# One pool of eight buffers for streamed weights and pair sums, free order of block products, and a new order of all steps

## The chip, the cores and the metric

The kernel runs on one core of a Trainium2 chip. The time is that of the core on the device, in microseconds (us), as the median of several executions. One further execution is recorded by the hardware profiler; all rows below come from that one.

## The reference

Eight batches of eight heads: 512 local rows that see a window of 32 to each side and 32 global rows, and 32 global rows that see everything. The result, as 4352 rows of 512, goes through an MLP with a gelu.

```python
k_all = np.concatenate([k_g, k_l], axis=2)
v_all = np.concatenate([v_g, v_l], axis=2)
s_g = scale * np.matmul(q_g, k_all.transpose(0, 1, 3, 2))
out_g = np.matmul(sm(s_g), v_all)
s_ll = scale * np.matmul(q_l, k_l.transpose(0, 1, 3, 2))
...
s_ll = np.where(mask, s_ll, -1000000000.0)
s_lg = scale * np.matmul(q_l, k_g.transpose(0, 1, 3, 2))
s_l = np.concatenate([s_lg, s_ll], axis=-1)
a_l = sm(s_l)
out_l = np.matmul(a_l, np.concatenate([v_g, v_l], axis=2))
return np.concatenate([out_g, out_l], axis=2).astype(np.float32)
...
h = x @ w_in
inv_sqrt2 = np.float32(1.0 / np.sqrt(2.0))
g = 0.5 * h * (1.0 + erf(h * inv_sqrt2))
return (g @ w_out).astype(np.float32)
```

Here `sm` is the softmax over the last axis, `w_in` is 512 x 2048 and `w_out` 2048 x 512.

## The kernel before

**Attention** is cut into 64 units: a batch, a half of its local rows, a pair of heads. A unit loads keys, queries and values (`load_k`, `load_q`, `load_v`: tiles `raws` and `vr`), transposes keys and queries, multiplies them on TensorE (`s`, line 906), masks and reduces on VectorE (line 925), takes the exponential on ScalarE (line 779, tile `a_t`), normalizes (`n`, tile `ge`), transposes the weights on TensorE (`t`, lines 980 to 983), copies them (`at`) and multiplies them by the values (`o`, line 1017). The global rows run beside it (`sg`, `gt`, `go`, `gx`, tiles `sgr`, `agt`, `gos`; their values come by `gu_load`, lines 1131 and 1133). Numbers of fp32 are cut into a high and a low part, so that a product is three matmuls: high by high, high by low, low by high. The low part is a subtraction, mostly on GpSimd (line 612).

**The MLP** takes 256 rows at a time: 16 chunks (a batch's half each) and one of all global rows. The first five are plain. The last twelve go in six pairs (index `k`), whose first layer is done by seven products of half-size blocks instead of eight (`i` = 1 to 7), for each quarter of the hidden columns (`q` = 0 to 3): 168 products, each of 12 matmuls of 128 x 256 (`ml_p`, line 1314, tile `hb`). The sums of weight blocks that the products want are made once (`sw`, `ss`, `sh`, `sl`), and written to DRAM with the plain blocks (`wd`, one tensor for each quarter). Each product then streams its weights back: step `rl` (`r_l`, line 1275) loads 128 x 1024 numbers into a tile `rt`, which is free again when the product has read it. Partial sums stand in PSUM (W, X, Y of a quarter); `cc` adds two of them into a tile `gq` for the gelu (line 779), and `gl`, the low part of the gelu's result, is the last to use it. The second layer (`mo`, lines 1360 to 1362, tile `acc`) adds up in two PSUM banks, and `ob` and `ow` copy and store the result.

**Buffers.** Sixteen large tiles of one pool hold half of the weights' high parts for good (eight) and serve as two rings of four: `rg` for `rt`, `gq` for pair sums (line 229). A ring hands out its oldest free buffer.

**What sets the order.** `graph()` names 4431 steps, each with what it needs, the buffers it takes and frees, and the engines that may run it. The order of all steps, and the engine of each, was found beforehand by a search and stands packed in the text `SEQ`: two bytes for a step, its number times six plus the engine. `plan()` unpacks it, and the loop at the end issues the steps in that order; each engine runs its own instructions in the order in which they are issued. The due times and the table `DUR` matter only to the search. Nearly all loads and stores are issued by SP (SyncE) in one queue; an instruction of SP that waits for a buffer holds all behind it. The products stand in a fixed order: each needs the one before it (`prev`, line 509), and each `rl` stands behind the one before it (`rprev`).

```python
ORDER = [(0, 1), (1, 1), (0, 2), (2, 1), (1, 2), (3, 1), (2, 2), (3, 2)] + [(q, i) for q in range(4) for i in (6, 5, 7, 3, 4)]
```

Of the kernel before, what the change touches and what calls it, by code (L numbers as in the profile page):

```python
# [139 lines left out]
FORMS = (3, 5, 7, 9, 11, 15, 19, 23, 27, 32)  # L140
# [17 lines left out]
    "8dM-oF@Ik0as!Mfq^Y{8xQr!93hIeiD8r{-%$CJA<2#y;=`OtLy3b2o8q+*{{G|tgmY&x8AL{_{F&S;5o#*zE|)UaeMuT{dydLa19s3J@ln;eMD3J&3b_UCeBfR-hUTIZ*}?o{yOwO^}^OD{vEKlo`Z)F9^r"
    "ua0`8Ju(>j4TTt5~^LbK3Ne6AircmvOE?Zo2=pMfcau)m5^v|jgP@ZI&c*0^7Y_q3W?1NDK{_Ieh<Oc3L<_%Fc|aew&@crIZwQHgisqpbmas$NI<3EWqoXw9}3@fkla(2H*({0c7mC)EF!=puYvKefKxItec"
    "hC<){7{q_BX7+^l}MS?0YrgebWkH7C<Km@ef@Pqgdi2L!c)~~JC1=bMf*N<-<sNYooE`AYlJKh{9l9u9!@t@$|uJ;pG5Z!^r^^;q-)Q1VX@f+|Ph(F-@;2rh80I0RUwU4x!@I2|;`pv``VFz({E2?!XemAj7"  # L160
    "I$Zw~{uKUYf|PujFq8BpVPET6e2TEYejjlHDI6#e#u5&-RtcB!2Z^r}Is=!8$6H?@?IO$}4YZ!9SCjQ*K54Y|EO8=Xc56CtuJsze5I9D3l7A<J$)m*E_<1A?`2l{2<Rgy_EGG2^mXp3Bfhi&Yg3?49A;ifyi"
    "1P_Ugq5UEN%LASw;mvzB-|n1Cdfz+h-V1z6E>2L5-^k-t$_N+#JhwqNFNi12@?ZU3Y>%`EodDf2`D<!{{<cq))C~yBNQNsNFq=cwK7OcTiL|_22x};1xSPtrIaFhW$OuwfLJB(C;dn=lGe1Uh!e<f2GGP&%7"
    "K85bey!Il|VdCdO2{Jax8F%GLHO^bdEAgIvKdr+CsWY`h(O?sv(C+4_fb%UL(H~cs-CJH4{GwtfuZG&jGEY-k^ZVO3Iejvw<hAFO#Q|ceFmB7%6^=jk1yIp$wA2fro+L0toW803y&u*-6Eb{|qq6B}%pCUSJ"
    "`aPo6;r1b-lZKpsQ+kqim$r%nW;g7_ddKp`(DuOgof{*O!vZl!J}M<^c#z9j!l{+2qPa+=Hv{!UI%c9Cz9CsU44FOVNo7(^g&8U;+9L0L(=9sD@3KJYjB1IjBD1ob$TK>dhvnmUj27KIcL(HQ{?QB9ZA_XDC"
    "pEOim(evnSRK$TIg^l{Yb0083#^)KqBppY7%KMk&?@PkG=m-<KWIqEvfrhuEcBk*-#UjV{*NWDs(ND~JilRb1TbqX~=R0d7dDE%q*bIOdMJ~%7*4JAz6K|wJ7kLsk77#?bXIybnF@-b~Ht(Ha%p=g~%E+bCQ"
    "QQN5%>Hrf@%Mw8$EMpvfFt`+$qB0l*)EP8Oa5j}n%hDONrA&Be5}h7;gNh3|X-%{tsw>E)i5M%HH-HO+O4@8@KfO#BhTfx&q3dW;#!T9Bs)hCn-NRTC^atlMwTyRYuhEv!-ej()nHYn#R@z2dg?IuKqP<98$"
    "ec&NK??_Yp&&yRTFs2nVvKljKf}TJlJ+YtP20rW#auui4))MS=zr1<GZxXu(WbC2(u%Zo%w4o4^!qejXqcV}ZexB<|Ad}n>|rJutAqQQJLnte&7tq<_Rw_J0BeNyI_m_Z7(76$Fb>gwqE~|#nB#&IgVTcRg1"
    "OMEp+3eU)@;`1pb6w+za4sxaf<E>9c7+k9;H2``Prki$BZ+~WuY_lw^*w}lNn1{A@--CVCX%@C3-*OHvJ98ON`%{A2Qw#Z3}J+%@6Gg*3c`V8}uQ@*w8R*4x>E;qoe2#=ua6*b~?0%wSl!IRAJLNG4>YLj?h"
    "ZR?$Ex_8phwu3*bYc;~^7kPw-&y5%Ve-$hrxJGVQE-`VXwn7{^$5!CM*sfMK;c_E(IfK{xAEki((TVJtxH`)$vLMj1g?9Sc)?o`I{~#u{PVV&Yk&AvWs|#wcrAh)W-CyUOTe-(~PQ0v3gJE~MZ{SpRFg98$B"
# [379 lines left out]
def attn_mlp(ctx, tc, q_l, k_l, v_l, q_g, k_g, v_g, w_in, w_out, out):  # L549
# [918 lines left out]
```

## Time and profile before

| | us |
|---|---|
| median of 3 runs | 1015.15 (1011.89 to 1018.85) |
| profiled execution | 1016.96 |
| its span, first to last instruction | 1015.2 |
| TensorE busy (PE) | 987.0, 97% |
| VectorE busy (DVE) | 745.0, 73% |
| ScalarE busy (ACT) | 715.9, 71% |
| GpSimd busy (POOL) | 444.9, 44% |

PE is matmuls, PEld the loading of their stationary side, SPq the queue of SyncE, which issues DMAs. A wait is idle time of an engine ahead of an instruction, put down to what ended last before it. The chain of waits follows the last instruction back, at each step to what released it. The granted clock is the share of TensorE's full clock that the chip gave it.

### The profile page before, as it was taken

How to read it: one execution, taken by the hardware profiler on the slowest of the kernel's cores; microseconds unless marked ns; L12 is line 12 of the kernel's file. 1: busy time of each engine (PE TensorE's matmuls, PEld its weight loads, DVE VectorE, ACT ScalarE, POOL GpSimd, SP SyncE). 2: the span in 40 equal slices, each digit the busy share in tenths (PEclk: the TensorE clock that was granted, in tenths of full speed). 3: DMA queues.
4: the chain of work that ended last, by engine and by line, in shares of the span. 5: the costliest groups of instructions: out<-in, count | busy, mean ns of one | idle time of the engine just before them, and what ended most of it. 6: DMA issues, size and time to landing. Idle time of an engine off the chain costs nothing.

```text
span 1015.2 us, 21336 instructions
## 1 busy us (share of the span) xinstructions
PE 987.0 (97%) x6712; PEld 865.3 (85%) x6712; DVE 745.0 (73%) x2184; ACT 715.9 (71%) x1703; POOL 444.9 (44%) x473
## 2 busy tenths in 40 slices
PE   7999999999999999999998999999999999999998
PEld 5767688998998888888897988888899979988986
DVE  5888999888898999788886886689888876231110
ACT  5888868778877688787776877777787766433231
POOL 6331657434344464244542464335533553325132
PEclk9999999999999999999999999999999999999999
DMA  9996322445545888876677657875678846754831
GB/s 216 291 273 153 65 49 45 110 89 156 130 89 154 241 242 267 239 195 147 179 211 204 140 141 197 235 210 139 176 201 244 218 96 200 247 167 122 265 113 42
DMA packets 307729, 175.06 MB, mean 172 GB/s; under 512 B 256256, under 2 KB 279040, under 8 KB 307616
## 3 DMA queue, kind: packets, MB, share of 16 engines
q1 hardware_dynamic: 304064, 171.07, 63.3%
q0 software_dynamic: 1344, 1.97, 0.7%
q8 instruction: 54, 0.88, 0.4%
q10 hardware_dynamic: 2208, 0.66, 0.3%
q14 instruction: 59, 0.48, 0.2%
HBM read 149.49 MB, written 24.12 MB: 171 GB/s over the span
## 4 chain that ended last, share of the span: by engine, by line
PE 71%; DMA 14%; DVE 8%; SPq 3%; ACT 2%; issue 2%; POOL 0%; DVEq 0%; ACTq 0%; POOLq 0%
PE hb L1314 18%; PE acc L1360 9%; PE acc L1361 9%; PE acc L1362 9%; DMA rt<-wd 4%; PE o L1017 4%; PE s L906 4%; PE h L1206 2%; PE h L1210 2%; PE t L980 2%; PE h L1211 2%; PE h L1212 2%; PE acc L1352 2%; DMA raws<-in_v_l_dram 2%; DMA raws<-in_q_l_dram 2%
## 5 line engine op out<-in xcount | busy, mean ns | idle before, releaser
L1360 PE MATMUL acc<-wh,gh 128*128 128x512 f32 x512 | 205.1, 401 | 0.0
L1361 PE MATMUL acc<-wh,gl 128*128 128x512 f32 x512 | 200.8, 392 | 1.1 <-POOL gl L612 1.0
L1362 PE MATMUL acc<-wl,gh 128*128 128x512 f32 x512 | 200.6, 392 | 0.0
L612 POOL TENSOR_TENSOR gl<-gf,gh 128x512 fp32r<-128x512 f32 x80 | 105.3, 1316 | 204.8 <-ACT gh L605 48.6
L1314 PE MATMUL hb<-fh,rt 128*128 128x256 f32 x960 | 183.4, 282 | 5.9 <-DMA rt<-wd 4.7
L1314 PEld LDWEIGHTS hb<-fh,rt 128*128 128x128 f32 x960 | 152.6, 189 | 10.4 <-DVE sm L925 2.6
L1314 PE MATMUL hb<-fl,rt 128*128 128x256 f32 x480 | 134.3, 280 | 0.0
L779 ACT ACTIVATE a_t<-a_t,sm 128x192 f32<-128x192 f32 (+1 forms) x256 | 117.1, 460 | 11.2 <-DVE sm L931 10.4
L1362 PEld LDWEIGHTS acc<-wl,gh 128*128 128x128 f32 x512 | 96.2, 188 | 21.1
L1360 PEld LDWEIGHTS acc<-wh,gh 128*128 128x128 f32 x512 | 96.7, 189 | 16.0 <-ACT ob L605 0.6
L1361 PEld LDWEIGHTS acc<-wh,gl 128*128 128x128 f32 x512 | 96.6, 189 | 16.1 <-POOL gl L612 1.7
L612 POOL TENSOR_TENSOR vs<-vr,vs 128x512 fp32r<-128x512 f32 x56 | 73.8, 1319 | 83.2 <-DVE k L612 13.0
L779 ACT ACT_TABLE_LOAD x69 | 88.5, 1283 | 16.2 <-PE acc L1362 6.5
L1314 PEld LDWEIGHTS hb<-fl,rt 128*128 128x128 f32 x480 | 90.4, 188 | 1.1
L925 DVE CUSTOM_DVE_ANT_0 a_t<-s,mask 128x192 f32<-128x192 f32 (+1 forms) x256 | 81.8, 366 | 11.0 <-PE s L906 10.2
L612 POOL TENSOR_TENSOR gl<-gq,gh 128x512 fp32r<-128x512 f32 x47 | 63.4, 1349 | 52.9 <-PE acc L1362 22.0
L605 ACT ACTIVATE at<-t 128x512 fp32r<-128x512 f32 (+1 forms) x112 | 59.0, 542 | 26.8 <-PE t L981 10.5
L1000 DVE TENSOR_TENSOR at<-t,at 128x512 fp32r<-128x512 f32 (+1 forms) x112 | 67.3, 615 | 14.0 <-ACT at L605 13.2
L1210 PE MATMUL h<-xh,wh 128*128 128x256 f32 x256 | 74.0, 289 | 0.9 <-DVE agt L1116 0.9
L1314 PE MATMUL hb<-xf,rt 128*128 128x256 f32 x576 | 74.8, 281 | 0.0
L1017 PE MATMUL o<-at,vs 128*128 128x256 f32 x448 | 70.3, 287 | 2.3 <-ACT sgr L779 1.6
L1314 PEld LDWEIGHTS hb<-xf,rt 128*128 128x128 f32 x576 | 71.1, 189 | 1.4
(196 smaller groups left out, 2348.0 us busy)
## 6 DMA issues: line engine op xcount, KB each, us to landing
rt<-wd SPq DMA_DIRECT2D x168, 512.0 KB, 4.6
wraw<-in_moe_w_in_dram SPq DMA_DIRECT2D x16, 512.0 KB, 6.1
wraw<-in_moe_w_out_dram SPq DMA_DIRECT2D x16, 512.0 KB, 6.2
raws<-in_v_l_dram SPq DMA_DIRECT2D x64, 128.0 KB, 4.0
out_dram<-ob SPq DMA_DIRECT2D x32, 256.0 KB, 3.0
raws<-in_k_l_dram SPq DMA_DIRECT2D x224, 36.0 KB, 2.8
raws<-in_q_l_dram SPq DMA_DIRECT2D x224, 32.0 KB, 3.1
vr<-in_v_l_dram SPq DMA_DIRECT2D x48, 128.0 KB, 4.1
```

What stands on the lines that cost most here:

```text
L605: nc.scalar.activation(out=out, in_=in_, func=AF.Copy)
L612: (nc.vector if e == "v" else nc.gpsimd).tensor_sub(**kw)
L779: nc.scalar.activation(func=func, **kw)
L906: nc.tensor.matmul(out=st[u, "s", jj][:, c:c + w], lhsT=qq[pr, qt * P:qt * P + P], rhs=kk[pr, k0:k0 + w], start=(i == 0 and n == 0), stop= ...
L925: nc.vector.tensor_tensor_reduce(out=a_t[:, j, aoff[half][i]:aoff[half][i] + w], in0=s[:, c:c + w], in1=masks[half][i], scale=1.0, scalar= ...
L1000: nc.vector.tensor_sub(out=at[:, 1], in0=st.pop((u, "t", j))[:, :n * P].rearrange("p (n q) -> p n q", q=P), in1=at.bitcast(F32)[:, 0])
L1017: nc.tensor.matmul(out=o[:, :, qsl], lhsT=l.rearrange("p s e -> p (s e)"), rhs=r, start=(n == 0), stop=(n == 3), skip_group_check=True)
L1210: nc.tensor.matmul(out=h, lhsT=hi, rhs=xh, start=(c == 0 and f % 2 == 0), stop=False, skip_group_check=True)
L1314: nc.tensor.matmul(out=h[:, r], lhsT=a, rhs=b, start=(i in (1, 5) and r == 0 and c == 0 and n == 0), stop=(c == 1 and n == 2), skip_group_ ...
L1360: nc.tensor.matmul(out=acc[t], lhsT=gh[:, f % 2, tsl], rhs=hi, start=(f == 0), stop=False)
L1361: nc.tensor.matmul(out=acc[t], lhsT=gl[:, f % 2, tsl], rhs=hi, start=False, stop=False)
L1362: nc.tensor.matmul(out=acc[t], lhsT=gh[:, f % 2, tsl], rhs=lo, start=False, stop=(f == NF - 1))
```

## The change

Four things. The two rings become one of eight buffers, `rg`, for the streamed weights and the pair sums (and for the weight sums before them). The products no longer need one another, nor the loads of weights, so that any order may be chosen in which each product has its data and its partial sums; those of a pair may overlap those of the next. Most loads and stores may be issued by SP or by GpSimd (`by(e)`). And the order of all steps is searched anew, with load times that were measured; of the text `SEQ` one line of each is shown. In the new order SP issues as many DMAs as before, 1350, and GpSimd none more. `FORMS` says which of the smaller tiles lie in which of two pools. `graph()` and the table `DUR` are otherwise as they were.

```diff
-FORMS = (3, 5, 7, 9, 11, 15, 19, 23, 27, 32)
+FORMS = (0, 1, 3, 11, 15, 19, 23, 25, 27, 32)
...
-    "c-jrriDME3<1k<bj2i}w`yMc0+&7H-8ZcnM7~>lE81tQGrl!8jpDi;pGh4RI%+#itnXj6fnVOj`H8nLgwPjv;rDkfTrl#Nb{1J}@YKInJqtF1<1LZ@%h9;pRXgl-@^f>f9Gz+ajWzat81ZWm^1FD6-3cU*j1"
...
+    "c-jrriDMFk;s9XAeP81m_kaQ8hH(uTFkrxd0b`77++%D{&6b(^me1BQGc#MZXJ%$LeP+wIY?+xYGh1qEYHHJ#&nq?4WoD+ProZ3!M|?Jz1(t*RU<sH2_5~~r7sFhzR@e#H6buYV!+wU9VCP|S*bG=NY#MeC{"
...
-    bufs = {"s": 2, "t": 2, "h": 2, "gg": 5, "u": 6, "sm": 4, "wr": NF, "fw": NF + 1, "rg": 4, "gq": 4}
+    bufs = {"s": 2, "t": 2, "h": 2, "gg": 5, "u": 6, "sm": 4, "wr": NF, "fw": NF + 1, "rg": 8}
...
-        rk = "gq" if g // 4 else "rg"
+        rk = "rg"
...
-            step(("ya", n), "y_a", (n,), "s", 270.0 + n, [("w5", n), ("w5", wl[-1])], [], [("fw", ("lo", n)), ("gq" if grp // 4 else "rg", ("H", grp))], issues=2, size=0.5)
+            step(("ya", n), "y_a", (n,), "sp", 270.0 + n, [("w5", n), ("w5", wl[-1])], [], [("fw", ("lo", n)), ("rg", ("H", grp))], issues=2, size=0.5)
...
-            step(("lv", u), "load_v", (u, 2), "s", f0 - 18.0, [("o", units[n - 2], 1)], [("vr0", u), ("vr1", units[n + 1])], issues=9, size=0.5, after=("lv", pu if n == NPV else units[n - 2]))
+            step(("lv", u), "load_v", (u, 2), "sp", f0 - 18.0, [("o", units[n - 2], 1)], [("vr0", u), ("vr1", units[n + 1])], issues=9, size=0.5, after=("lv", pu if n == NPV else units[n - 2]))
...
-                step(("glv", g, i), "gu_load", (g, i), "s", g0 - 12.0 + 2 * i, [("tk", units[NPE - x]) for x in (3, 4)], [("gvr", (g, i))], issues=6, size=0.33, after=("glv", *pi) if pi[0] else None)
+                step(("glv", g, i), "gu_load", (g, i), "sp", g0 - 12.0 + 2 * i, [("tk", units[NPE - x]) for x in (3, 4)], [("gvr", (g, i))], issues=6, size=0.33, after=("glv", *pi) if pi[0] else None)
...
-        prev = ("P", k - 1, 3, 4) if k else ("hc", keys[NPL - 1], NF - 1, NCC - 1)
-        rprev = ("rl", k - 1, 3, 4) if k else None
...
-            step(("rl", k, q, i), "r_l", (k, q, i), "s", Q - 9.0, w, [("rg", (k, q, i))], issues=1, size=0.52, after=rprev)
-            rprev = ("rl", k, q, i)
-            step(("P", k, q, i), "ml_p", (k, q, i), "t", Q, [prev, ("rl", k, q, i), ("fl", k, i)] + more, [W[q]] if i == 1 else [Y[q]] if i == 5 else [],
-                 [("rg", (k, q, i))] + ([] if q < 3 else [("xx%d" % x, (k, "F")) for x in (2 * i - 2, 2 * i - 1)] if i < 3 else [("fw", ("F", k, i, x)) for x in range(2)]))
-            prev = ("P", k, q, i)
+            step(("rl", k, q, i), "r_l", (k, q, i), "sp", Q - 9.0, w, [("rg", (k, q, i))], issues=1, size=0.52)
+            step(("P", k, q, i), "ml_p", (k, q, i), "t", Q, [("rl", k, q, i), ("fl", k, i)] + more, [W[q]] if i == 1 else [Y[q]] if i == 5 else [],
+                 [("rg", (k, q, i))] + ([("xx%d" % x, (k, "F")) for x in (2 * i - 2, 2 * i - 1)] if i < 3 else [("fw", ("F", k, i, x)) for x in range(2)]))
...
-                step(("se", k, q), "ml_se", (k, q), "a", Q - 1.0, [("sd", k, q), ("P", k, q - 1, 3) if q else ("P", k, 3, 2)], [X[q]], [("s1%d" % q, k)])
+                step(("se", k, q), "ml_se", (k, q), "a", Q - 1.0, [("sd", k, q)], [X[q]], [("s1%d" % q, k)])
...
-                step(("cc", k, q), "ml_cc", (k, q), "v", Q + 1.5, [("P", k, q, 7), ("qc", k, q)], [("gq", (k, q))], [("q", (k, q))])
+                step(("cc", k, q), "ml_cc", (k, q), "v", Q + 1.5, [("P", k, q, 7), ("qc", k, q)], [("rg", (k, q))], [("q", (k, q))])
...
-                step(("gl", key, f), "ml_gl", (key, f), "v" if key == "g" and f == NF // 2 - 1 else "p", d + 1.3, [("gh", key, f)], [("gl", (key, f))], [("gq", (k, q)) if bh else ("gf", (key, f))])
+                step(("gl", key, f), "ml_gl", (key, f), "v" if key == "g" and f == NF // 2 - 1 else "p", d + 1.3, [("gh", key, f)], [("gl", (key, f))], [("rg", (k, q)) if bh else ("gf", (key, f))])
...
-    spare = {"fw": [2 * NF - 1], "rg": [], "gq": []}
+    spare = {"fw": [2 * NF - 1], "rg": []}
...
+    def by(e):
+        return {"a": nc.scalar, "p": nc.gpsimd, "s": nc.sync}[e]
...
-            st["S", g] = room("gq" if g // 4 else "rg", ("S", g), [P, 4, CH], F32, "ss")
+            st["S", g] = room("rg", ("S", g), [P, 4, CH], F32, "ss")
...
-        nc.sync.dma_start(out=t.bitcast(F32), in_=wd[q][:, FORM[i]])
+        by(e).dma_start(out=t.bitcast(F32), in_=wd[q][:, FORM[i]])
...
-        st["gq", k, q] = t = room("gq", (k, q), [P, 2, 2, CH], F32, "gq")
+        st["gq", k, q] = t = room("rg", (k, q), [P, 2, 2, CH], F32, "gq")
```

The table `SEQ` sets the order; two places show what it does.

SP's queue at the loads for the fourth quarter (`wd3`) of the second pair. Among them stand `raws` (keys, line 726, and queries, line 731; with lines 1131 and 1133 values for the global rows). Before, with `rt_7891` for product 6, `rt_8039` for product 5 and the others for 7, 3 and 4:

```order
L1275 DMA rt_7889<-wd2_125 128x1024
L1275 DMA rt_7891<-wd3_126 128x1024
L726 DMA raws_142<-in_k_l_dram 32x9x32 x4
L1131 DMA raws_142<-in_v_l_dram 128x4x64 x2
L1133 DMA raws_142<-in_v_g_dram 32x2x64 x4
L1275 DMA rt_8039<-wd3_126 128x1024
L731 DMA raws_142<-in_q_l_dram 32x8x32 x4
L1275 DMA rt_8053<-wd3_126 128x1024
L1275 DMA rt_8074<-wd3_126 128x1024
L1275 DMA rt_8101<-wd3_126 128x1024
```

After, with `rt_7852` for product 5, `rt_7908` for product 6, and `wd0` for the first weights of the next pair:

```order
L1274 DMA rt_7852<-wd3_126 128x1024
L1274 DMA rt_7854<-wd2_125 128x1024
L730 DMA raws_142<-in_q_l_dram 32x8x32 x4
L1274 DMA rt_7908<-wd3_126 128x1024
L725 DMA raws_142<-in_k_l_dram 32x9x32 x4
L1274 DMA rt_8076<-wd3_126 128x1024
L1274 DMA rt_8085<-wd3_126 128x1024
L730 DMA raws_142<-in_q_l_dram 32x8x32 x4
L1274 DMA rt_8137<-wd0_123 128x1024
L1181 DMA xg_136<-gc_8053 128x32
L1274 DMA rt_8169<-wd3_126 128x1024
```

The weights of product 5 stood behind four loads of keys and six of values for the global rows, and now stand first of their quarter; of values nothing stands among them any more, and weights of the next pair come ahead of the quarter's last.

ScalarE's queue at the last unit of attention, where the exponentials (`a_t`, `sgr`) and the gelus (`gf`, `gq`) alternate. Before:

```order
L779 ACTIVATE gf<-hb 128x512
L779 ACT_TABLE_LOAD
L779 ACTIVATE a_t_128,sm<-a_t_128,sm 128x192
L779 ACTIVATE a_t_128,sm<-a_t_128,sm 128x224
L779 ACTIVATE sgr_132,gsm<-sgr_132,gsm 128x544
L605 ACTIVATE vs<-vr 128x8x64
L605 ACTIVATE hb<-s_5278 128x512
L779 ACTIVATE a_t_128,sm<-a_t_128,sm 128x192
L779 ACTIVATE a_t_128,sm<-a_t_128,sm 128x224
L779 ACT_TABLE_LOAD
L779 ACTIVATE gf<-hb 128x512
```

After:

```order
L778 ACT_TABLE_LOAD
L778 ACTIVATE gf<-hb 128x512
L601 ACTIVATE hb<-s_5316 128x512
L601 ACTIVATE q<-hb 128x512
L601 ACTIVATE gh<-gf 128x512
L778 ACT_TABLE_LOAD
L778 ACTIVATE sgr_132,gsm<-sgr_132,gsm 128x544
L601 ACTIVATE xf<-xb 128x256 x2
L778 ACT_TABLE_LOAD
L778 ACTIVATE gq<-hb 128x512
L778 ACTIVATE gf<-hb 128x512
```

Exponentials that stood in one run between two table loads are now cut by a gelu, which makes three table loads in eleven rows instead of two. Over the whole kernel ScalarE has 80 table loads instead of 70, and VectorE 2223 instructions instead of 2186 (casts of `gh` and low parts of weights above all, taken from ScalarE and GpSimd).

## Rows read from the trace of the kernel before

**Rows 1.** Page, part 1: busy us (share of the span) x instructions, by engine

```profile
PE 987.0 (97%) x6712; PEld 865.3 (85%) x6712; DVE 745.0 (73%) x2184; ACT 715.9 (71%) x1703; POOL 444.9 (44%) x473
```

**Rows 2.** Busy us (x instructions) by stage: PE, PEld, DVE, ACT, POOL, clock, DMA

```profile
0.00:150.00 150.00, 140.11 (x815) 105.73 (x816) 123.36 (x362) 118.92 (x288) 67.55 (x110) 1.00 0.69 176
150.00:350.00 200.00, 199.84 (x1449) 180.98 (x1449) 176.29 (x516) 154.47 (x380) 95.08 (x98) 1.00 0.49 121
350.00:850.00 500.00, 487.05 (x3457) 435.67 (x3456) 410.91 (x1233) 386.80 (x924) 231.01 (x227) 1.00 0.74 195
```

**Rows 3.** Waits of TensorE, 350 to 850 us: total us, times, longest

```profile
PE hb L1314 <- DMA rt<-wd: 4.7, 5, 2.1
PE t L980 <- ACT gq L779: 1.9, 1, 1.9
PE o L1017 <- ACT sgr L779: 1.6, 1, 1.6
PE acc L1361 <- POOL gl L612: 1.0, 1, 1.0
PE gx L1166 <- DVE gos L1161: 0.8, 1, 0.8
PE t L980 <- ACT gf L779: 0.8, 2, 0.6
```

**Rows 4.** Streamed weights' tile rt: issue ns min/median/max; landing us

```profile
L1275 SPq DMA_DIRECT2D rt<-wd x168: 319/371/1643, 334.5 to 971.9; - x168
...
DMA to landing us min/median/max: 3.4/4.6/7.7
```

**Rows 5.** Waits of SP's queue, whole span: total us, times, longest

```profile
SPq L1275 <- PE hb L1314: 110.8, 71, 10.5
```

**Rows 6.** Chain of waits, 524 to 556 us: start us, us, what

```profile
538.39 7.12 DMA rt<-wd
...
546.90 3.87 DMA rt<-wd
```

**Rows 7.** Timeline, 538 to 552 us: start us, us, what [idle before, releaser]

```profile
540.94 0.63 ACT L605 ACTIVATE vs<-vr 128x512 fp32r<-128x512 f32 x1 [3.06 <-DMA rt<-wd]
...
541.59 1.28 ACT L779 ACT_TABLE_LOAD   x1
...
542.88 0.60 ACT L779 ACTIVATE gq<-hb 128x512 f32<-128x512 f32 x1
543.01 3.79 SPq L1133 DMA_DIRECT2D raws<-in_v_g_dram  x4
...
543.53 0.44 PE L980 MATMUL t<-ident,a_t 128*128 128x128 f32 x2 [1.86 <-ACT gq L779]
...
546.90 0.37 SPq L1275 DMA_DIRECT2D rt<-wd  x1
...
550.90 0.36 PE L1314 MATMUL hb<-fh,rt 128*128 128x256 f32 x1 [2.06 <-DMA rt<-wd]
```

**Rows 8.** Busy us by single microseconds from 552; clock is behind POOL

```profile
552.00:553.00 1.00, 1.00 (x7) 1.00 (x6) 0.31 (x3) 0.00 (x0) 0.00 (x0) 0.52 1.01 381
553.00:554.00 1.00, 1.00 (x7) 1.00 (x6) 0.18 (x1) 0.41 (x1) 0.00 (x0) 0.50 1.03 410
554.00:555.00 1.00, 1.00 (x4) 0.80 (x4) 0.90 (x4) 0.76 (x2) 0.00 (x0) 0.50 1.02 414
555.00:556.00 1.00, 1.00 (x5) 0.82 (x4) 0.97 (x4) 0.98 (x2) 0.00 (x0) 0.77 1.02 414
```

**Rows 9.** Groups of ScalarE, 350 to 850 us: busy us, mean ns, idle

```profile
L779 ACT ACT_TABLE_LOAD x42 | 53.9, 1283 | 10.5 <-PE acc L1362 6.3 <-PE hb L1314 2.4 <-issue 1.2
```

**Rows 10.** Chain of waits, whole span, two pieces: start us, us, what

```profile
613.02 7.12 DMA raws<-in_v_l_dram
...
806.28 6.70 DMA out_dram<-ob
```

**Rows 11.** Waits of TensorE, first 150 us

```profile
PE qp L827 <- DMA raws<-in_q_l_dram: 4.4, 2, 4.3
```

More of the change, by code (lines that the diff above doesn't have):

```diff
@@ L318, in graph @@
             if n >= NPE:
-                step(("lg", b), "load_g", (b,), "s", s0 - 12.0, takes=[("kgr", b)], issues=4, size=0.03, after=("lq", units[n - 2]) if n == NPE else ("lg", b - 1))
-            step(("lh", b), "load_h", (b,), "s", s0 - 12.0, [("q2", pu)] if n > NPE else [], [("kq", ("g", b))], issues=4, size=0.03, after=("lk", u) if not n else ("lh", b - 1))
+                step(("lg", b), "load_g", (b,), "sp", s0 - 12.0, takes=[("kgr", b)], issues=4, size=0.03, after=("lq", units[n - 2]) if n == NPE else ("lg", b - 1))
+            step(("lh", b), "load_h", (b,), "sp" if n else "s", s0 - 12.0, [("q2", pu)] if n > NPE else [], [("kq", ("g", b))], issues=4, size=0.03, after=("lk", u) if not n else ("lh", b - 1))
             step(("tg", b), "st_tg", (b,), "v", s0 - 6.0, [("lh", b)])
@@ L333, in graph @@
             last = [("tq", units[NPE - x]) for x in (3, 4)] if n < NPE + 2 else []
-            step(("lk", u), "load_k", (u,), "s", s0 - 15.0, last, [("kraw", u)], issues=4, size=0.2, after=pu and ("lk", pu if n > NPE else units[n - 2]))
-            step(("lq", u), "load_q", (u,), "s", s0 - 14.0, last, [("qraw", u)], issues=4, size=0.18, after=pu and ("lq", pu if n > NPE else units[n - 2]))
+            step(("lk", u), "load_k", (u,), "sp", s0 - 15.0, last, [("kraw", u)], issues=4, size=0.2, after=pu and ("lk", pu if n > NPE else units[n - 2]))
+            step(("lq", u), "load_q", (u,), "sp", s0 - 14.0, last, [("qraw", u)], issues=4, size=0.18, after=pu and ("lq", pu if n > NPE else units[n - 2]))
             step(("tk", u), "st_tk", (u,), "v", s0 - 5.0, [("lk", u), ("lg", b), ("q2", pu) if n > NPE else None, ("tgl", b)], [("kq", (u, "k"))], [("kraw", u), ("kgr", b)])
@@ L427, in LO @@
         g = 2 * (f // 4) + f % 2
-        return [("fw", ("lo", 2 * f)), ("gq" if g // 4 else "rg", ("H", g))] if key == keys[NPL - 1] else []
+        return [("fw", ("lo", 2 * f)), ("rg", ("H", g))] if key == keys[NPL - 1] else []
     for n, key in enumerate(keys):
@@ L730, in load_q @@
         for j, pr, es in quads():
-            nc.sync.dma_start(out=qraw[pr], in_=q_l[b, 2 * p + j].rearrange("(c r) e -> r c e", r=32)[:, 8 * half:8 * half + 8, es])
+            by(e).dma_start(out=qraw[pr], in_=q_l[b, 2 * p + j].rearrange("(c r) e -> r c e", r=32)[:, 8 * half:8 * half + 8, es])
     def load_g(e, b):
```

172 lines of the change are left out of this document (86 added, 86 removed).

## The prediction

> **What bounds the kernel now.** I read four views in this order: the busy times by engine, the same by stage, the waits of TensorE, and then the DMA side of the longest of them. TensorE is busy for 987.0 of the span's 1015.2 us [rows 1], so 28.2 us of idle time is nearly all that a new order of the same work can win; the order has the same 6514 TensorE instructions before and after. By stage [rows 2] the idle time lies in three places: 9.9 us in the first 150 us (weights and first heads arrive), 0.2 us from 150 to 350, 12.95 us from 350 to 850 (attention beside block products), and so 5.2 us after 850, which is mostly the last store. The middle stage is the one to look at, since the streamed weights live there. Its longest waits are 4.7 us in five pieces for a load of weights (rt), 1.9 us for a gelu, 1.6 us for an exp of the global rows, 1.0 us for a low part from GpSimd [rows 3]. A weight load lands 4.6 us after its issue in the median, 7.7 us at worst, and its issue costs SP 0.37 us but up to 1.64 [rows 4].
>
> Why are they late? SP issues in order, and its longest wait by far is weight loads that wait for a product to leave their buffer: 110.8 us in 71 waits [rows 5]. Everything behind such a load stands too. The stretch from 538 to 551 shows it: the chain runs through two weight loads, 7.12 and 3.87 us long, with one product between them [rows 6]. In the timeline SP issues two weight loads, then keys, then six pieces of values for the global rows, the last four of which take it 3.79 us, and only at 546.90 the next weights; TensorE starts that product at 550.90 after 2.06 us of waiting. ScalarE meanwhile had stood 3.06 us before a copy of values, so that a table load and the gelu ran late and the transposes waited 1.86 us [rows 7]. The price goes on after the wait: TensorE had idled for these 1.86 and 2.06 us within ten, and from 552 on the granted clock is 0.52 and 0.50, the lower of its two levels (1.2 instead of 2.4 GHz), until 556 [rows 8].
>
> **The change part by part.**
>
> *Eight shared buffers.* Counted in the order, every one of the 164 loads of the old kernel that reuse a buffer takes one that a product left, with exactly three products between that one and the one that reads the load. In the new order 141 loads take a buffer left by a product: 88 have more than three products between, 23 three, 30 fewer; the other 27 take buffers left by pair sums or by the first weights. Counted along TensorE's order, 25 loads have fewer than 70 matmuls between release and use where 62 had, and the median goes from 80 to 111; at the middle's 487.05/3457 = 0.141 us for one [rows 2] 70 are 9.9 us. For the five products that waited (found by counting the products up to the wait) the three products between become five, seven, four, thirteen, and once a buffer left by a pair sum. So I take the 4.7 us as gone, and put back what loads with three or fewer between cost so far: 4.7 over 164 is 0.029 us each, for 53 of them 1.5 us. Bounds: 0 (all have time) to 4.7.
>
> *Loads behind weight loads on SP.* Three more waits hang on late transfers: the gelu's 1.9 us (above); the 1.0 us for the low part, at 630, in a stretch whose chain runs through a load of values of 7.12 us that held SP's next loads; and the exp's 1.6 us, which follows a store of 6.70 us that ScalarE's next buffer waited for [rows 10]. They are 4.5 us together. In the order shown in the section on the change, the four-piece load no longer stands between the weights of one quarter. I count the 4.5 us as won; bounds 0 and 4.5, nearer to the upper since two of three hang on SP's queue, which 8 buffers relieve.
>
> *The clock.* At 0.52, 0.50, 0.50 and 0.77 [rows 8] the four us from 552 to 556 lost 0.48, 0.50, 0.50 and 0.23 us, together 1.7. The idling before it was the two waits that I take as gone, so this comes back: -1.7, bounds 0 and -1.7, and +1.7 for each new stretch like it.
>
> *Ten more table loads.* ScalarE's row has 80 instead of 70. Each is 1.283 us [rows 9], so 12.8 us are added on an engine that is idle for 299 us [rows 1]. What hides them is that TensorE rarely waits for ScalarE: in the middle 1.9 + 1.6 + 0.8 = 4.3 us for its gelu and exp [rows 3], with 42 table loads there [rows 9], so 0.1 us for each. Ten cost 1.0; bounds 0 and 12.8 where each stands on the path. In the row the gelu starts at 542.88, straight after the table load from 541.59 [rows 7]. The Trainium skill (ScalarE: Activation LUTs, What ACT_TABLE_LOAD costs) puts a switch at about 1283 ns plus 1380 ns of draining, by which ten would hold ScalarE for 26.6 us; the trace agrees on the first part and shows no second here.
>
> *Steps moved to VectorE.* Its row grows from 2186 to 2223. At its mean of 745.0/2184 = 0.34 us that is 12.6 us on an engine that is idle for 270 [rows 1]; beside the 410.91 of 500 us in the middle [rows 2] there is room. I take 0, and 12.6 is the price if the cover were gone. Loads may now be issued by GpSimd, but the order puts none there (1350 issues on SP before and after), so this part costs nothing. The places of tiles in memory and the dropped order of products by themselves issue nothing.
>
> *The rest of the order* is dealt anew everywhere. The first stage starts with the same first query load; I take 0 there with 3 us either way, and the last store is unchanged.
>
> Sum: -4.7 + 1.5 - 4.5 - 1.7 + 1.0 = -8.4 us. The profiled execution took 1016.96 us, so 1008.6 in its terms; it lies 1.8 us above the median of the runs, which gives **1006.8 us**, 0.8% below 1015.15.
>
> **The rivals.**
>
> *The waits change places.* TensorE is 97% full, and a wait taken away exposes the next late step: the next two rows are already lined up at 0.8 us [rows 3]. If the new order closes as tightly as the old one, the 12.95 us return under other names and the time is about 1015, from 1010 to 1020. For it: the whole order is new, so every small wait is drawn again. Against it: the weight loads were the only wait that came five times.
>
> *Loads crowd each other, and it gets slower.* Thirty loads now have fewer than three products between release and use, and with more buffers up to seven loads can be in flight. A load that comes late costs 4.7/5 = 0.94 us. To end 1% above the old time, the gain of 8.4 and another 10.2 us must be paid: about 20 late loads. If all thirty wait it is 28.2 instead of 1.5: -9.9 + 28.2 = +18, about 1033. For it: landing times already spread from 3.4 to 7.7 us [rows 4], and the engines are at 0.74 of their time in the middle [rows 2]. Against it: the count under 70 matmuls falls from 62 to 25, since more other work now lies between products. The Trainium skill (DMA: Bandwidth & Descriptors, Issuing engines are not separate DMA queues) says that all transfers end on the same 16 engines and interleave, which speaks for this rival: an earlier weight load takes its time from a load of keys or values beside it. No row of before shows seven in flight, so it stays a chance, not a term.
>
> *More than the loads is won.* If the search also closes the other middle waits, 12.95 + 1.7 us go, and of the first stage's 9.9 us at most 5.5 (4.4 waits for the first query loads [rows 11]). That gives 1016.96 - 14.7 - 1.8 = 1000, down to 995.
>
> *It doesn't do what it says.* That can be set aside: the order shows both the freed order of products and the wider ring in use; only the freedom to issue from GpSimd is unused.
>
> **How the numbers follow.** About 1% is what a measurement of this kernel can tell from no change (the three runs span 0.7%). Chances: the forecast 0.48 (1001 to 1012), waits change places 0.22 (1010 to 1020), more than the loads 0.18 (994 to 1003), crowding 0.12 (1019 and up). One per cent faster is under 1005.0: nearly all of the third case and half of the forecast's, 0.16 + 0.24 = 0.40. One per cent slower is over 1025.3: 0.09, most of the last case. The rest, 0.51, is within 1%. The range 996 to 1019 leaves out most of the crowding and the lower end of the third case, less than 0.2 together. Its lower end holds the bound of all middle waits, its upper end that of ten bare table loads less the weights' gain (1016.96 - 1.8 - 8.4 - 1.0 + 12.8 = 1018.6).
>
> **What would show it.** Right: TensorE's idle time from 350 to 850 falls from 12.95 to about 6 us; waits for rt fall to 2 us or less; SP's wait on products falls to less than half of 110.8 us; no stretch at the lower clock level in the middle; ten more table loads of 1283 ns with hardly more waits for ScalarE. Wrong: waits for rt as long as before at other products (crowding), with a median landing over 5.5 us; or the waits for rt gone and those for gelu, at and gl grown by as much (the waits changed places); or a first stage that is more than 3 us longer or shorter.

## The result and the profile after

| | before | after |
|---|---|---|
| median, us | 1014.18 (4 runs, 1011.89 to 1018.85) | 1000.65 (4 runs, 999.72 to 1002.62) |
| profiled execution, its span | 1016.96, 1015.2 | 999.72, 997.9 |

The ratio is 0.9863, 95% interval [0.9824, 0.9903]: 13.9 us of 1015 by the ratio, 13.5 by the medians. The forecast was 8.4 us less; 1000.65 lies in the range of 996 to 1019, just under the forecast's own band (1001 to 1012) and in that of the third rival ("more than the loads is won", 994 to 1003). More than one per cent faster had the chance 0.40.

The stages of the kernel after, columns as in [rows 2], then TensorE's waits from 350 to 850 us (all of them; total us, times, longest), as [rows 3]:

```profile
0.00:150.00 150.00, 143.31 (x836) 108.72 (x837) 127.39 (x389) 118.66 (x291) 59.84 (x100) 1.00 0.69 179
150.00:350.00 200.00, 199.43 (x1445) 181.19 (x1443) 171.99 (x519) 154.32 (x373) 95.04 (x100) 1.00 0.51 128
350.00:850.00 500.00, 495.79 (x3552) 447.21 (x3551) 409.72 (x1252) 395.89 (x937) 233.22 (x230) 1.00 0.76 201
850.00:997.90 147.90, 143.18 (x885) 128.53 (x883) 33.29 (x63) 44.42 (x86) 47.60 (x40) 0.99 0.48 150
```

```profile
PE s L905 <- DVE gc L1177: 1.0, 1, 1.0
PE hb L1313 <- ACT s L601: 0.9, 1, 0.9
PE s L905 <- DVE agg L1124: 0.7, 1, 0.7
PE s L905 <- DVE at L999: 0.5, 1, 0.5
PE o L1016 <- DVE at L999: 0.3, 1, 0.3
PE hb L1313 <- DVE sgr L1075: 0.2, 1, 0.2
PE sg L1062 <- DVE xb L1048: 0.2, 1, 0.2
PE hb L1313 <- ACT hb L601: 0.2, 1, 0.2
```

TensorE's idle time falls from 9.89 to 6.69 us in the first 150 us and from 12.95 to 4.21 in the middle stage. There the waits for rt, for the gelu's `gq`, for the exp's `sgr` and for the low part `gl` of [rows 3] are all gone; what is left is none over 1.0 us. In windows of 2 us the granted clock is 1.00 all through the middle stage, unlike [rows 8] (the stage's mean is 1.00 in both profiles and doesn't tell). Waits of other engines for transfers went with them: in the middle stage VectorE waited 9.1 us for loads of queries before (`qt`) and ScalarE 5.9 us for stores of results (`at`), and after neither has such a wait. The page's busy row, the tile rt, SP's longest wait and the table loads of the middle stage answer to [rows 1, 4, 5, 9], in this order:

```profile
PE 981.7 (98%) x6712; PEld 865.7 (87%) x6712; DVE 742.4 (74%) x2221; ACT 713.3 (71%) x1682; POOL 435.7 (44%) x467
```

```profile
L1274 SPq DMA_DIRECT2D rt<-wd x168: 319/376/1451, 331.4 to 952.1; - x168
...
DMA to landing us min/median/max: 3.3/4.4/7.0
```

```profile
SPq L1274 <- PE hb L1313: 85.1, 49, 5.7
```

```profile
L778 ACT ACT_TABLE_LOAD x51 | 65.4, 1283 | 10.4 <-PE acc L1361 4.8 <-DVE sm L930 3.1 <-issue 1.7
```

Three things do not fit the prediction. SP still waits 85.1 us for products, which is not less than half of 110.8, and 10.9 us more for `gl`, which frees the pair sums that now share the ring. ScalarE, with 51 table loads in the middle stage instead of 42, makes TensorE wait 1.1 us there (0.9 and 0.2 above) instead of 4.6 (the 4.3 of the prediction and 0.3 for a copy). And the first stage has 3.2 us less idle time, more than the 3 us that the prediction names as a sign of being wrong.

### The profile page after: what moved, and what is told of

It reads as the page before. It is cut to its first block, busy times and chain, and to the rows that moved or that the text cites. A ratio compares the mean times of both kernels' runs of the same rounds, so it can differ in the third digit from the quotient of the medians.

```text
span 997.9 us, 21322 instructions
## 1 busy us (share of the span) xinstructions
PE 981.7 (98%) x6712; PEld 865.7 (87%) x6712; DVE 742.4 (74%) x2221; ACT 713.3 (71%) x1682; POOL 435.7 (44%) x467
## 4 chain that ended last, share of the span: by engine, by line
PE 80%; DMA 7%; DVE 5%; ACT 3%; SPq 3%; issue 1%; POOL 1%; DVEq 0%; POOLq 0%; ACTq 0%
PE hb L1313 20%; PE acc L1359 10%; PE acc L1360 10%; PE acc L1361 10%; PE o L1016 4%; PE s L905 4%; PE acc L1351 3%; PE h L1209 3%; PE h L1210 3%; PE h L1211 3%; DMA wraw<-in_moe_w_out_dram 2%; PE h L1205 2%; PE t L979 2%; PE go L1149 2%; DMA rt<-wd 1%
## 5 line engine op out<-in xcount | busy, mean ns | idle before, releaser
L778 ACT ACT_TABLE_LOAD x79 | 101.4, 1283 | 12.4 <-PE acc L1361 4.8
L608 POOL TENSOR_TENSOR vs<-vr,vs 128x512 fp32r<-128x512 f32 x56 | 73.7, 1315 | 77.2 <-DMA raws<-in_v_g_dram 9.4
L608 POOL TENSOR_TENSOR vgs<-raws,vgs 128x640 fp32r<-128x640 f32 x32 | 50.5, 1578 | 72.6 <-DMA raws<-in_q_l_dram 29.5
```

The source lines that it names most:

```text
L608: (nc.vector if e == "v" else nc.gpsimd).tensor_sub(**kw)
L778: nc.scalar.activation(func=func, **kw)
```

## The experiments

The theory: weight loads come earlier, because a ring of eight lets them stand earlier in SP's queue without holding it. First rival: the new order does it, whatever the buffers. The kernel before had medians of 1014.75, 1016.91, 1017.91 and 1017.10 us beside runs 1 to 4, 5 to 8, 9 to 11 and 12, so kernels are compared by their ratio to it, and differences in us are ratios times 1015. A difference between two rows carries the intervals of both, 3 to 5 us for most of them.

| run | median us | ratio, 95% interval | us against before | SP waits for products, us |
|---|---|---|---|---|
| after | 1000.65 | 0.9863 [0.9824, 0.9903] | -13.9 | 85.1 |
| 1 pool alone | 1012.83 | 0.9982 [0.9963, 1.0001] | -1.8 | 81.9 |
| 2 new order, rings of 4 | 1030.82 | 1.0159 [1.0132, 1.0186] | +16.1 | 129.0 |
| 3 old order, then new | 1006.0 | 0.9914 [0.9894, 0.9934] | -8.7 | 84.4 |
| 4 new order, then old | 1011.32 | 0.9968 [0.9947, 0.9989] | -3.2 | 85.1 |
| 5 twenty more table loads | 1028.49 | 1.0129 [1.0103, 1.0156] | +13.1 | 87.5 |
| 6 old order, earliest loads | 1154.85 | 1.1381 [1.135, 1.1412] | +140.2 | 224.9 |
| 7 old order, early loads | 1050.12 | 1.0349 [1.0321, 1.0378] | +35.4 | 134.6 |
| 8 new order, late loads | 1009.68 | 0.9942 [0.9924, 0.9961] | -5.9 | 73.7 |
| 9 old order, six loads moved | 1016.07 | 0.9979 [0.9957, 1.0001] | -2.1 | 83.8 |
| 10 casts as before | 1002.93 | 0.9866 [0.9837, 0.9895] | -13.6 | 83.3 |
| 11 more casts on VectorE | 1003.9 | 0.9873 [0.9844, 0.9902] | -12.9 | 79.5 |
| 12 short pieces on ScalarE | 1009.27 | 0.9913 [0.9879, 0.9947] | -8.8 | 86.8 |

**Run 1: the ring alone.** The text `SEQ` of before in the kernel after, and

```diff
-FORMS = (0, 1, 3, 11, 15, 19, 23, 25, 27, 32)
+FORMS = (3, 5, 7, 9, 11, 15, 19, 23, 27, 32)
```

> The changed kernel with the old order of all steps (and the old places of the small tiles): only the ring of eight is new. Weight loads stand where they stood in SP's queue, but the buffer that each takes has been free for longer. Theory 'lead' (the weights come earlier because a load no longer waits for the product three before its own): SP's wait on products falls from 110.8 us to under 60, TensorE's waits for rt from 4.7 to 2 or less, the waits that hung on loads behind them shrink too, and the time is 1005 to 1010. Rival 'order' (a newly drawn order closes the gaps, whatever the buffers): 1012 to 1016, with waits for gelu, exp and low parts as before.

The ring by itself wins 1.8 us, hardly more than nothing, and the interval includes nothing. SP waits 28.9 us less for products, and TensorE still waits for weights, as the waits of the middle stage show:

```profile
PE hb L1313 <- DMA rt<-wd: 3.8, 5, 2.2
```

The loads stand at the same places in SP's queue, behind the same loads of values. The theory in its plain form ("a freer buffer is an earlier load") falls by its own numbers. The time is the rival's, but its waits are not: those for the gelu's `gq`, for `sgr` and for `gl` of [rows 3] are gone from this profile, whose middle stage idles 7.7 us instead of 12.95. Its first stage, in the same order as before, idles 12.4 us instead of 9.9 and has two stretches at the lower clock (12 to 18 and 68 to 76 us). One profile of each kernel doesn't tell how much of the middle stage's gain stays; the medians say 1.8 us.

**Run 2: the new order without the ring.** Two rings of four, so the loads must be later; each stands where the old ring would let it, and all lines that name the rings are those of before:

```diff
-    bufs = {"s": 2, "t": 2, "h": 2, "gg": 5, "u": 6, "sm": 4, "wr": NF, "fw": NF + 1, "rg": 8}
+    bufs = {"s": 2, "t": 2, "h": 2, "gg": 5, "u": 6, "sm": 4, "wr": NF, "fw": NF + 1, "rg": 4, "gq": 4}
...
         order.append(x)
+    P = [x["name"][1:] for x in order if x["name"][0] == "P"]
+    loads, out, n, m = {}, [], 0, 0
+    for x in order:
+        if x["name"][0] == "rl":
+            loads[x["name"][1:]] = x
+        else:
+            out.append(x)
+            n += x["name"][0] == "P"
+        while m < len(P) and m < n + 4 and P[m] in loads:
+            out.append(loads[P[m]])
+            m += 1
+    order = out
```

> The changed kernel with two rings of four again, its order kept but for the weight loads: each moves later in the list, to behind the fourth product before its own, where it would come earlier. Theory 'lead': waits for rt come back, 4 to 10 us of them in the middle stage, SP's wait on products exceeds 100 us, and the time is 1005 to 1012. Rival 'order': within 2 us of 1000.65, with no wait for rt over 1 us.

Neither expectation came. It is 30 us slower than with the ring, far more than the waits for weights account for (1.1 us in the middle stage). SP's queue from 522 us (timeline), the chain of waits there, and TensorE's longest wait show what happens:

```profile
522.75 6.95 SPq L1286 DMA_DIRECT2D rt<-wd x5
529.79 1.87 SPq L742 DMA_DIRECT2D raws<-in_q_l_dram  x4
```

```profile
527.94 1.43 PE hb L1325 x12
...
529.38 0.32 SPq L1286
...
531.21 4.11 DMA raws<-in_q_l_dram
...
535.88 0.59 DVE at L1011
...
536.51 1.12 PE gt L1119 x4
```

```profile
PE gt L1119 <- DVE at L1011: 4.8, 1, 4.8
```

Five weight loads hold SP for 6.95 us; the last starts when a product ends at 529.37. Only then do four query loads go out. They land 4.1 us after the last of them, VectorE transposes them and only then makes `at`, and TensorE has stood 4.8 us. Here the price of a late weight load is paid by the load behind it. This is one wait of 20.6 us of idle time in the middle stage; what the others hang on is not shown.

**Run 8: the same late places with the ring of eight**, that is the `plan()` lines of run 2 alone.

> The changed kernel with its ring of eight and its order, but each weight load moved to behind the fourth product before its own, as in the run with rings of four (1030.8 us). The loads stand at the same late places of SP's queue, but find a free buffer more often. If the 30 us there came from SP standing for a buffer while loads of keys, queries and values wait behind it: SP's wait on products falls from 129 to under 70 us and the time is 1003 to 1012. If they came from the weights being issued late: 1020 to 1031, as there.

The time is the theory's; SP waits 73.7 us instead of 129.0, a little over its 70, and 22.0 us of the 30 are back. The smaller ring of the pair sums is not the cause of these: in run 2 as in run 8 VectorE has no wait for a pair sum's buffer in the middle stage. The other 8.0 us (0.9942 against 0.9863, with 4.4 us either way) are what the loads' earlier places are worth in the new order. Only 1.2 us of run 8's waits in the middle stage are for weights themselves; 3.2 us are for copies by ScalarE (`hb`), the most for any step. So within this order the ring is worth 22 us with the loads at late places, and the early places another 8 us.

**Runs 6 and 7: the old order with early loads.** `full` counts the buffers in use at each step; the last line but one says + 0 in run 6, + 10 in run 7:

```diff
+        j = i
+        while j - 1 > lo and full[j - 1] < 8:
+            j -= 1
+        j = min(i, j + 0)
+        order.insert(j, order.pop(i))
```

> The old order with the ring of eight, and each weight load moved to the earliest place in the list at which the ring has a free buffer, at most eight products ahead. The median load then stands five products ahead of its own in the list, instead of two. Theory 'place in SP's queue' (the ring helps only when the loads stand early enough to use it): waits for rt vanish, the gain comes without the new order, 1003 to 1008. Rival 'rest of the order' (the other steps had to move too): 1010 to 1015, waits under other names. If SP now stands for buffers as long as before (over 100 us), the loads of keys and values behind are late, and the time is 1015 or more.

> As the run before, but each weight load ten places of the list behind the earliest one, so that its buffer is mostly free when SP comes to it; the median load stands three products ahead. Theory 'place in SP's queue': waits for rt under 1 us, SP's wait on products under 70 us, 1003 to 1008, and no worse than the run with the earliest places. Rival 'rest of the order': 1010 to 1015.

Both end on the wrong side; in run 6 the last case of its expectation came. In run 6 SP's waits and the middle stage are

```profile
SPq L1299 <- PE hb L1338: 224.9, 87, 7.1
SPq L1299 <- POOL gl L633: 46.1, 13, 8.3
```

```profile
350.00:850.00 500.00, 423.69 (x2775) 375.05 (x2775) 333.06 (x997) 314.26 (x750) 185.74 (x182) 0.92 0.62 163
```

No wait of TensorE for rt is left in either, and in run 6 TensorE is idle for 76 us of 500, at a mean clock of 0.92. Other transfers are late instead: in the middle stage VectorE waits 16.3 us for keys (`kt`; 1.2 before) and ScalarE 34.6 us for stores of results (`at`; 5.9 before). In the old order an early place costs more than it wins where SP must stand for the buffer.

**Run 9: six loads ahead of what stood before them**, in the kernel of run 1, where the ring has a free buffer:

```diff
+EARLIER = {(0, 1, 4): ("lv", (3, 1, 2)), (0, 2, 5): ("lh", 4), (1, 2, 4): ("lv", (5, 0, 0)), (1, 3, 5): ("glv", (4, 0), 1),
+           (2, 1, 5): ("glv", (5, 1), 0), (2, 3, 5): ("gw", (5, 0), 1)}
...
+    for r, ahead in EARLIER.items():
+        names = [x["name"] for x in order]
+        order.insert(names.index(ahead), order.pop(names.index(("rl",) + r)))
```

> The old order with the ring of eight, and six weight loads a few places earlier in SP's queue, ahead of the loads and stores of attention that stood before them, where the ring already has a free buffer; they are the loads for which TensorE waited in the run with the ring alone (3.8 us in five waits, 5.3 us with the small ones). All else is as in that run. If a wait for weights is worth its length, as the prediction took it: no wait for rt over 0.5 us, and 4 to 5 us less, 1007.5 to 1009. If the gap comes back under another name: 1012 to 1014.

The gap came back under other names: the ratio is that of run 1. The waits of the middle stage:

```profile
PE hb L1318 <- ACT hb L606: 2.5, 1, 2.5
PE hb L1318 <- DMA rt<-wd: 2.4, 3, 0.9
PE t L984 <- ACT gq L783: 1.7, 1, 1.7
PE o L1021 <- ACT sgr L783: 1.0, 1, 1.0
```

The long wait for weights (2.2 us in run 1) is gone, and a copy that is late by 2.5 us stands in its place, beside a gelu and an exp that TensorE waited for before, but not in run 1. A single wait is not worth its length here.

**Runs 3 and 4: which part of the order.** The first 1523 steps (to about 312 us, before any weight is streamed) from one order, the rest from the other; run 4 has the two names exchanged:

```diff
+    codes = list(read(OLD))[:1523]
+    done = set(v // 6 for v in codes)
+    codes += [v for v in read(SEQ) if v // 6 not in done]
```

> The changed kernel with the old order for the first 1523 steps (up to about 312 us, before the first weight is streamed) and the new order for the rest. Theory 'lead': most of the gain lies in the streamed part and stays; the 3 us that the new order's first stage wins are lost, 1003 to 1005. If the first stage won more than its idle time shows, 1008 or more.

> The mirror of the run before: the new order for the first 1523 steps, then the old one, with the ring of eight. Theory 'lead': the gain of the ring alone and the 3 us of the first stage together, so 3 us under the run with the ring alone, 1002 to 1007. Rival 'order': 1010 to 1012, the 3 us of the first stage and nothing else.

Run 3 falls between its two cases (by the ratio 1006.4), run 4 on its rival's. With the ring in all four, the new streamed part is worth 6.9 us behind the old start (runs 1, 3) and 10.7 behind the new one (run 4, after); the new start 1.4, which its interval does not tell from nothing, and 5.2. (Run 1 alone of the four has the old `FORMS`.) The gain of ring, start and streamed part taken singly is 1.8 + 1.4 + 6.9 = 10.1 us of 13.9; the remaining 3.8 is no more than the intervals leave open. The first stage with the old start (run 3) and the new one (run 4):

```profile
0.00:150.00 150.00, 138.85 (x804) 104.69 (x805) 122.94 (x352) 118.27 (x288) 65.72 (x108) 0.99 0.68 176
```

```profile
0.00:150.00 150.00, 143.23 (x836) 108.44 (x837) 127.58 (x389) 118.67 (x291) 59.93 (x101) 1.00 0.69 179
```

**Runs 5 and 12: what ScalarE's time costs.** Ahead of ten gelus, an exp of one column (run 5), so that the table is changed twice, or six copies of one column (run 12):

```diff
     def ml_g(e, key, f, *way):
+        if (key, f) in EXTRA:
+            act(AF.Exp, out=tiny, in_=ident[:, 0:1])
```

```diff
     def ml_g(e, key, f, *way):
+        if (key, f) in EXTRA:
+            for i in range(6):
+                act(AF.Copy, out=tiny, in_=ident[:, 0:1])
```

> The changed kernel with an exp of one column ahead of ten gelus of the middle stage, each between two gelus that shared a table: twenty more table loads on ScalarE, at 1.283 us 25.7 us of its time. At the price taken in the prediction, 0.1 us each, the time is 2 us longer, about 1003. If each stood on the path, 1026; half of them, 1013.

> The changed kernel with no table load more, but six copies of one column, 0.203 us each, ahead of the same ten gelus as in the run with twenty more table loads: 12.2 us of ScalarE's time in pieces of 1.22 us, about as long as one table load, where that run put pieces of 2.77 us. If ScalarE's time counts one for one at these places: 12 us more, 1011 to 1015. If the order leaves about a table load's length of slack ahead of a gelu and only longer pieces reach TensorE: 0 to 4 us more, 1000 to 1005.

Run 5 is 27.0 us slower than after (1.0129 against 0.9863), for 20 x 1.283 + 10 x 0.203 = 27.7 us of ScalarE: one for one in the sum, though not place by place. One of the ten places in the timeline of run 5, ScalarE, then TensorE, then the clock by single microseconds (behind POOL):

```profile
403.81 1.28 ACT L779 ACT_TABLE_LOAD   x1
405.11 0.20 ACT L779 ACTIVATE tiny<-ident 128x1 f32<-128x1 f32 x1
405.33 1.28 ACT L779 ACT_TABLE_LOAD   x1
406.62 0.60 ACT L779 ACTIVATE gq<-hb 128x512 f32<-128x512 f32 x1
...
407.42 0.59 ACT L602 ACTIVATE hb<-s 128x512 f32<-128x512 f32 x1
```

```profile
408.07 0.58 PE L1316 MATMUL hb<-fh,rt 128*128 128x256 f32 x1 [3.02 <-ACT hb L602]
```

```profile
408.00:409.00 1.00, 0.93 (x4) 0.94 (x5) 0.55 (x2) 1.00 (x4) 0.00 (x0) 0.50 0.46 89
...
413.00:414.00 1.00, 1.00 (x6) 1.00 (x5) 1.00 (x9) 0.27 (x1) 0.00 (x0) 0.50 1.03 359
```

The copy `hb<-s`, which stands behind the gelu, is late by the 2.77 us put in; the product that wants it waits 3.02 us, and from 408 to 414 the granted clock is 0.50, the lower level, which costs another 3 us. So this place costs by an estimate 6 us; others cost less (behind the exp at 628.35 TensorE waits 1.2 us). Over the middle stage TensorE is idle for 22.8 us instead of 4.2, in a profiled execution that is 6.8 us above its median. Run 12 has 12.2 us in shorter pieces and costs 5.1 us by the ratios (8.6 by the medians), idle 9.3 us instead of 4.2 in the middle stage. So neither expectation held alone: a piece of one table load's length costs 0.5 to 0.9 us at these places in the mean, with an interval that by the ratios just includes nothing (5.1 us, 5.3 either way); one of two table loads 2.7.

**Runs 10 and 11: casts.** In `plan()`, with `SWAP` 50 steps `gh` (run 10: the engines of before) or 17 of them (run 11: these from ScalarE to VectorE):

```diff
+    for x in order:
+        if x["name"][0] == "gh" and x["name"][1:] in SWAP:
+            x["on"] = {"a": "v", "v": "a"}[x["on"]]
```

> The changed kernel with all casts of the gelu's result on the engines that they had before: 33 from VectorE to ScalarE and 17 the other way, so 16 more casts of 0.63 us, 10 us, on ScalarE. By the prediction's term (nothing for steps moved to VectorE, since ScalarE is idle for 28% of the time): within 2 us of 1000.65. By what the twenty table loads cost (28 us for 25.7 us of ScalarE's time): 1009 to 1013.

> The changed kernel with 17 more casts of the gelu's result on VectorE instead of ScalarE, which has 10.7 us less to do and VectorE 7 us more. If ScalarE's time goes into the span one for one in both directions: 990 to 994. If only work that is added in the wrong place costs, since the order has been fitted to what is there: 999 to 1003, and slower where a cast now stands behind VectorE's own work.

Both are as fast as after within the intervals: ScalarE's busy time is 724.6 and 706.4 us instead of 713.3, so 11.3 us more and 6.9 less, and the ratio changes by 0.0003 and 0.0010. ScalarE's total is not what counts. Its casts differ from the pieces of run 5 in place, in length (0.63 us against 2.77) and in being moved from one engine to another, not added. Run 12 speaks for the length; which of the three counts is not shown.

## Why the prediction came out as it did

The direction and the main stage were right; the sum was too small by 5 us, and one of its reasons was wrong. The range is 23 us wide and holds the old time too, so that the new time lies in it says little for the terms.

*Weight loads, -4.7 + 1.5.* The 4.7 us went; the 1.5 us put back were not paid, since no wait for rt is left. But the argument behind them, products between release and use, does not carry the gain: run 1 has the ring and keeps 3.8 us of waits, run 9 shortens them and gains nothing, runs 6 and 7 remove them and lose 35 to 140 us. What the runs show is that ring and order work together: the order puts loads early (8.0 us, run 8), and the ring keeps SP free where it does (22.0 us, runs 2 and 8). In one row: the ring alone wins 1.8 us, the new order with late loads 4.1 on top of it (run 8 against run 1), the early places 8.0.

*Loads behind weight loads, -4.5.* Right in kind: the three waits are gone, in the profile of run 1 too, and run 2 shows the mechanism on one chain. Its sign, SP's wait under half of 110.8, was wrong: runs 1 and 4 have 81.9 and 85.1 us, as after has, and are 12 and 11 us slower. SP may stand as long as nothing urgent is behind it; the total does not tell where it stands.

*The clock, -1.7.* Right for the two profiled executions: no low stretch in the middle after. Run 5 has five new ones there, behind waits of 1.9 to 3.0 us, though none behind one of 1.90 us at 374.8. Over all executions the term is too small: the mean granted clock of before is 0.9956 over the 66 executions beside runs 1 to 12 and that of after 0.9988 over its four, an estimated 3 us of 1015. In the profiles part of that lies in the first stage, where the term looked for none: five of the six with the old start have a low stretch there, three of the eight with the new one.

*Ten more table loads, +1.0.* The step failed in its working. Waits divided by loads gave 0.1 us each; a load put at a place that was not made for it cost 1.4 in run 5, and copies of a load's length 0.5 to 0.9 (run 12). The new order pays nothing visible for its ten, as its waits for ScalarE fell from 4.6 to 1.1 us: they stand where ScalarE is not awaited, and that was not to be read from an average. The Trainium skill (ScalarE: Activation LUTs, What ACT_TABLE_LOAD costs) adds about 1380 ns of draining to a switch, by which an estimate has the 20 switches of run 5 hold ScalarE for 53 us. The trace does not agree: in run 5 the exp starts 0.02 us after its load ends and the gelu 0.01 us after its own, and the kernel is 27.0 us longer; the measurement decides for 1283 ns alone.

*Steps moved to VectorE, 0.* Right as far as the casts go (runs 10 and 11); no run shows it for the low parts taken from GpSimd.

*The first stage, 0 with 3 us either way.* Mis-sized: 3.2 us less idle in the profile, 1.4 to 5.2 us by runs 3 and 4, with 3 to 5 us either way. The profiles bear it out: the first 150 us have 9.9 to 12.4 us of idle time in the six with the old start and 6.7 to 8.9 in the eight with the new one. The 4.4 us for the first query loads stand in both; gone are waits for VectorE (1.7, 1.0 and 0.9 us). No run tells which of its steps brings it.

With 1.5 not put back, 1.0 not paid and 3.2 for the first stage the sum is -8.4 - 1.5 - 1.0 - 3.2 = -14.1, against -13.5 to -13.9 measured. That it closes is in part luck. The terms are read from the two profiled executions, and these lie 17.2 us apart, one above its median and one below. Their spans differ by 17.3 us: 12.0 of idle time, 8.7 of it in the middle and 3.2 in the first stage, and 5.3 of busy time of the same 6712 matmuls. Of the latter the clock's stretch is 1.7, and the other 3.6 no term names. Nor are the terms shown to be separate: run 9 says that they are not.

*The rivals.* "Waits change places" did not come for the whole change, but is what single edits of the old order do (run 9). "Loads crowd each other" did not come: the median landing is 4.4 us against 4.6, the longest 7.0 against 7.7. "More than the loads is won" came, in the middle and in the first stage both.

## What to carry to other kernels

Where one queue issues all transfers in order, as SP does here, look at what stands behind a transfer that waits for a buffer (4.8 us of TensorE in run 2). A larger ring was worth what it freed in that queue, and that only together with an order that uses it. In a schedule that is full to 98%, price an added piece by the slack at its own place, not by an engine's idle share: 11 us more of ScalarE cost nothing as short casts moved to it, 28 us cost 27 as table switches ahead of gelus. And to credit a gain, cross the parts (old and new order, with and without the ring): single edits of the old order would have said that the ring is worth 1.8 us.

## What was not expected of the hardware

ScalarE's waits stand mostly ahead of the table load, not between it and the activation. In the kernel after, 12 of 79 table loads have over 0.25 us of idle time beside them, 8 ahead and 4 behind. One of the 8 in the timeline (idle time and its releaser in brackets):

```profile
479.53 1.28 ACT L778 ACT_TABLE_LOAD   x1 [2.09 <-PE acc L1361]
480.83 0.60 ACT L778 ACTIVATE gf<-hb 128x512 f32<-128x512 f32 x1
```

So waiting hid a switch at most 4 times of 79. ScalarE's idle time is also in small pieces; its longest waits of the middle stage in the kernel after are (total, times, longest)

```profile
ACT sgr L1068 <- PE sg L1062: 10.8, 10, 3.2
...
ACT L778 <- DVE sm L930: 3.1, 1, 3.1
...
ACT gos L1156 <- PE go L1149: 2.6, 1, 2.6
```

Of all its waits there, two exceed the 2.77 us that run 5 put in. And in a kernel that waits often the clock adds to the loss: in run 6 the mean granted clock of the middle stage is 0.92, so by an estimate 424 us of busy time there did the work of about 390.
